# Fused attention and gated feed-forward on one core: maxima and sums of the read path in one operation for both head groups, under a new order of emission

## The chip, the cores and the metric

The kernel runs on one core of one Trainium2 chip. The metric is device time in microseconds of one execution. Before the change it is 356.61 us, the median of 3 runs (355.37 to 356.98). Engines are named as the profile names them: PE (TensorE), PEld (its weight loads), DVE (VectorE), ACT (ScalarE), POOL (GpSimd), SP (the queue that issues most transfers).

## What is computed

The reference works on x (8 batches, 8 heads, 512 positions, 64 columns) and a state of 32 rows for each batch and head, and then on both together (544 rows of 512 columns a batch) in a gated feed-forward layer:

```
scores = scale * x @ state^T ; a = softmax(scores) over the 32 state rows
xread  = a @ state
scores2 = scale * state @ x^T ; a2 = softmax(scores2) over the 512 positions
sread  = a2 @ x
y = concat([xread, sread]) with the heads side by side   # (8, 544, 512)
h = relu(y @ w_in)                                       # 1024 columns
c = convolution of 3 taps along the 544 rows, column by column
out = (h * sigmoid(c)) @ w_out
```

Softmax subtracts the row's maximum, and adds 1e-9 to the sum before it divides. The "read path" of this document is sread: the softmax over the 512 positions and its product with x.

## The kernel before

**Tiles.** A batch's scores stand transposed: 128 partitions are 4 heads of 32 state rows each, and the 8 heads make NG = 2 head groups of 512 positions. `at_b` holds both groups (128 x 2 x 512). The x path's softmax runs down the partitions in blocks of 32 on a transposed copy (`att_flip` to `att_back`); the read path's runs along the 512 positions: `top` takes each row's maximum (line 340), `exp2` the exponential with the sum as a by-product (346), `norm2` adds 1e-9 and takes the reciprocal (349, 350), `flip` and `flipped` transpose the exponentials for `read` (the product with x, 368), `divide` scales the result (375), `read_flip` and `read_flipped` put it into `sr` (379, 383). From there `state_hidden` (615) and `state_relu` (619) make the hidden columns of the state rows of four batches at a time, eight pieces f.

**The feed-forward part.** For batches 1 to 7 the hidden columns of the positions come as the product of the attention weights with (state @ w_in), in split precision: each of `a` and `u` is a high and a low part, 6 matmuls of 128x512 a piece (`hidden`, 630). Batch 0 is done in plain float32 in two halves of 256 positions (`first_scores`, `first_flip`, `first_shift`, `first_exp`, `first_sum`, `first_spread`, `first_hidden`, lines 320 and 488 to 523 and 637). `relu`, the taps `middle`, `before`, `behind` (673, 678), `sigmoid`, `gate`, `gate_high` and `gate_low` follow, and `project` (713 for two pieces of batch 0, 705 for the others) multiplies by `w_out`, 3 matmuls for each 128 positions.

**Weights.** `w_in` and `w_out` arrive as 64-bit floats in 16 pieces of 512 KB; ACT (`w_abs` 243, `w_round` 246) and DVE (`w_shift` 249, `w_sum` 252, `w_sign` 260) make 32-bit floats of each. `w_load(8)` to `w_load(15)` are the pieces of `w_out`; ACT and DVE then split them (`w_high`, `w_low`). The name in the order is `raw_j` for piece j, and `hc_j` for what `w_abs` makes of it.

**What sets the order.** Every step is added to a plan as one operation with an engine, the tokens it reads and those it writes. ORDER is a table of operation numbers; the plan emits the operations in that row. A negative number -n stands for n filler matmuls on zeros (line 215), a `v` behind a number puts an operation that ACT or DVE could do on DVE. Each engine works through its operations in the row's order and waits for the tiles that they need; a tile's buffer comes free when its last reader is done. `xx`, the x tile of `read`, has one buffer (1024 KB a batch, `x_load`, 302), `xt` four (512 KB, `xt_load`, 298), PSUM eight banks in turn. SP issues transfers in order too: one that waits holds those behind it.

Of the kernel before, what the change touches and what calls it, by code (L numbers as in the profile page):

```python
# [953 lines left out]
```

## Time and profile before

| what | value |
|---|---|
| median of 3 runs | 356.61 us |
| span of the profiled execution | 354.1 us |
| PE busy | 348.6 us (98%) |
| PEld busy | 271.8 us (77%) |
| DVE busy | 316.1 us (89%) |
| ACT busy | 256.1 us (72%) |
| granted TensorE clock, mean | 1.000 |
| transfers | 35.06 MB, mean 99 GB/s |

Busy time counts from an instruction's start to its end; instructions of one engine overlap a little, so sums of durations come out somewhat above the time that passes. The profile's chain follows the work that ended last back to the start, at each step to what released it. Stretches of the span are read on their own: the first 60 us hold the weights' conversion, batch 0 and nearly all loads, the rest is feed-forward work with the attention of later batches between it.

### The profile page before, as it was taken

How to read it: one execution, taken by the hardware profiler on the slowest of the kernel's cores; microseconds unless marked ns; L12 is line 12 of the kernel's file. 1: busy time of each engine (PE TensorE's matmuls, PEld its weight loads, DVE VectorE, ACT ScalarE, POOL GpSimd, SP SyncE). 2: the span in 40 equal slices, each digit the busy share in tenths (PEclk: the TensorE clock that was granted, in tenths of full speed). 3: DMA queues.
4: the chain of work that ended last, by engine and by line, in shares of the span. 5: the costliest groups of instructions: out<-in, count | busy, mean ns of one | idle time of the engine just before them, and what ended most of it. 6: DMA issues, size and time to landing. Idle time of an engine off the chain costs nothing.

```text
span 354.1 us, 6694 instructions
## 1 busy us (share of the span) xinstructions
PE 348.6 (98%) x2538; PEld 271.8 (77%) x2538; DVE 316.1 (89%) x563; ACT 256.1 (72%) x560; POOL 29.4 (8%) x90
## 2 busy tenths in 40 slices
PE   7999999999999999999999999999999999999995
PEld 6766758876788868878789887878788868888884
DVE  1999999999999999999999999987799898889950
ACT  3999999998777997859856657774745447548642
POOL 1000000010000000100000300042201001113000
PEclk9999999999999999999999999999999999999999
DMA  7989998201600033030400000001200011000205
GB/s 255 396 309 377 328 357 302 62 1 50 219 0 2 0 127 142 3 119 32 180 30 2 0 31 31 30 3 60 89 2 0 0 71 65 2 2 0 74 33 176
DMA packets 13584, 35.06 MB, mean 99 GB/s; under 512 B 1520, under 2 KB 4720, under 8 KB 12528
## 3 DMA queue, kind: packets, MB, share of 16 engines
q1 hardware_dynamic: 12976, 34.28, 27.1%
q8 instruction: 20, 0.33, 0.4%
q10 hardware_dynamic: 576, 0.35, 0.3%
q14 instruction: 12, 0.10, 0.1%
HBM read 25.71 MB, written 8.91 MB: 98 GB/s over the span
## 4 chain that ended last, share of the span: by engine, by line
PE 97%; DMA 2%; ACT 0%; SPq 0%; issue 0%
PE acc L705 47%; PE ps_h L630 22%; PE ps_h L637 4%; PE ps_hs L615 4%; PE ps_u L548 4%; PE acc_t L705 3%; PE ps_r L368 2%; PE ps_t L355 2%; PE ps_s L310 2%; DMA xt<-xT 2%; PE acc_c L705 2%; PE acc L713 2%; PE ps_u L567 1%; PE ps_s L498 1%; PE ps_x L498 1%; PE ps_x L512 1%
## 5 line engine op out<-in xcount | busy, mean ns | idle before, releaser
L705 PE MATMUL acc<-wo,g 128*128 128x512 f32 x726 | 177.0, 393 | 0.0
L705 PEld LDWEIGHTS acc<-wo,g 128*128 128x128 f32 x726 | 134.7, 188 | 32.8 <-issue 1.7
L630 PE MATMUL ps_h<-a,u 128*128 128x512 f32 x336 | 83.2, 391 | 0.0
L630 PEld LDWEIGHTS ps_h<-a,u 128*128 128x128 f32 x336 | 62.7, 188 | 13.1
L682 ACT ACTIVATE t<-t 128x512 f32<-128x512 f32 x64 | 39.9, 630 | 14.5 <-DVE t L678 14.3
L673 DVE SCALAR_TENSOR_TENSOR t<-h,cw,t 128x511 f32<-128x511 f32 x64 | 47.1, 742 | 1.6 <-ACT t L194 1.5
L678 DVE SCALAR_TENSOR_TENSOR t<-h,cw,t 128x512 f32<-128x512 f32 (+1 forms) x64 | 46.8, 745 | 0.6
L205 ACT ACTIVATE g<-t 128x512 fp32r<-128x512 f32 (+1 forms) x62 | 37.5, 615 | 11.0 <-DVE t L687 5.5
L687 DVE SCALAR_TENSOR_TENSOR t<-t,h 128x512 f32<-128x512 f32 (+1 forms) x64 | 42.4, 667 | 2.3 <-ACT t L682 2.2
L208 DVE TENSOR_TENSOR g<-t,g 128x512 fp32r<-128x512 f32 (+1 forms) x62 | 41.3, 671 | 3.5 <-ACT g L205 3.1
L194 ACT ACTIVATE t<-h,cw 128x512 f32<-128x512 f32 x52 | 36.9, 723 | 4.3 <-DVE h L202 3.0
L200 ACT ACTIVATE h<-ps_h 128x512 f32<-128x512 f32 x56 | 33.3, 596 | 9.3 <-PE ps_h L630 6.1
L648 POOL COPY h<-hs 128x1 f32<-128x1 f32 x40 | 14.2, 376 | 129.2 <-ACT sr L383 66.3
L205 ACT ACTIVATE u<-ps_u 128x512 fp32r<-128x512 f32 x28 | 16.2, 596 | 8.5 <-PE ps_u L548 8.5
L719 ACT ACTIVATE o<-acc 128x512 f32<-128x512 f32 (+1 forms) x30 | 15.8, 544 | 8.5 <-PE acc L705 8.3
L648 POOL COPY hs<-h 128x1 f32<-128x1 f32 x40 | 13.6, 361 | 97.6 <-ACT h L200 80.9
L208 DVE TENSOR_TENSOR u<-ps_u,u 128x512 fp32r<-128x512 f32 x28 | 18.6, 682 | 2.5 <-ACT u L205 2.5
L615 PEld LDWEIGHTS ps_hs<-sr,wi 128*128 128x128 f32 x128 | 14.8, 192 | 1.1 <-ACT t L194 0.8
L637 PE MATMUL ps_h<-p,u 128*128 128x256 f32 x64 | 15.3, 386 | 0.0
L615 PE MATMUL ps_hs<-sr,wi 128*128 128x128 f32 x128 | 15.0, 276 | 0.0
L548 PE MATMUL ps_u<-wi,st 64*32 64x512 f32 x224 | 14.3, 597 | 0.0
L637 PEld LDWEIGHTS ps_h<-p,u 128*128 128x128 f32 x64 | 11.6, 190 | 3.3 <-DVE hc L249 0.8
(99 smaller groups left out, 400.3 us busy)
## 6 DMA issues: line engine op xcount, KB each, us to landing
xt<-xT SPq DMA_DIRECT2D x16, 512.0 KB, 7.7
xx<-xn SPq DMA_DIRECT2D x8, 1024.0 KB, 5.9
out<-o SPq DMA_DIRECT2D x27, 256.0 KB, 2.1
raw<-w_in SPq DMA_DIRECT2D x8, 512.0 KB, 7.6
raw<-w_out SPq DMA_DIRECT2D x8, 512.0 KB, 7.4
out<-o SPq DMA_DIRECT2D x6, 128.0 KB, 1.8
out<-o_t SPq DMA_DIRECT2D x8, 64.0 KB, 1.7
st<-stT SPq DMA_DIRECT2D x1, 448.0 KB, 10.2
```

What stands on the lines that cost most here:

```text
L194: A.activation(dst, src, AF.Copy, scale=scale)
L200: A.activation(dst, src, AF.Relu, scale=0.5)
L205: A.activation(hi, src, AF.Copy)
L208: engine.tensor_tensor(lo, src, hi.bitcast(F32), op=ALU.subtract)
L615: PE.matmul(ps_hs[m, f][:, :NT], wi[:, k, f * P:(f + 1) * P], sr[m][:, k, :], start=(k == 0), stop=(k == NK - 1))
L630: PE.matmul(ps_h[i], u[j][:, g, fs], a[k][:, g, :], start=(n == 0), stop=(n == 3 * NG - 1))
L637: PE.matmul(ps_h[f][:, q * HS:(q + 1) * HS], us[0, f // 4][0][:, g, f % 4 * P:(f % 4 + 1) * P], half_of(pa[0], q)[:, g, :], start=(g == 0) ...
L673: V.scalar_tensor_tensor(t[:, 1:], h[:, :S - 1], cw[:, f, 0:1], t[:, 1:], op0=ALU.mult, op1=ALU.add)
L678: V.scalar_tensor_tensor(t[:, :n], h[:, 1:n + 1], cw[:, f, 2:3], t[:, :n], op0=ALU.mult, op1=ALU.add)
L682: A.activation(tt[i], tt[i], AF.Tanh, scale=0.25)
L687: V.scalar_tensor_tensor(tt[i][:, :n], tt[i][:, :n], 1.0, hd[i][:, :n], op0=ALU.add, op1=ALU.mult)
L705: PE.matmul(acc, g[j][:, cs], wo[:, k, f, :], start=(f == 0 and n == 0), stop=(f == NF - 1 and n == 2))
```

## The change

`top` and `norm2` now take both head groups of a batch in one operation: `nm2` and `s2` are tiles of two columns, one a group, and the maximum runs over `at_b` as a whole (128 x 2 x 512 to 128 x 2). `exp2` and `divide` stay one a group and read and write a column of them. With that the plan has 24 instructions fewer on DVE, the operations behind have other numbers, and ORDER is a new table.

```diff
-0 98 99 100 101 102 103 120 -9 123 121 125 -3 124 -1 142 143 126 2 -2 150 3 127 5 20 4 144 151 128 6 -1 152 132 145
+0 98 99 100 -2 101 -3 102 103 -2 120 123 125 -1 121 -2 140 2 124 126 3 141 142 143 14 -1 127 5 148 149 -1 4 144 6 15
...
-    def top(i):
-
-        b, g = divmod(i, NG)
-        nm2[i] = buf([P, 1], F32, "nm2", f"nm2_{i}")
-        V.tensor_reduce(nm2[i], at[b][:, g, :], axis=AX.X, op=ALU.max, negate=True)
+    def top(b):
+        nm2[b] = buf([P, NG], F32, "nm2", f"nm2_{b}")
+        s2[b] = buf([P, NG], F32, "s2", f"s2_{b}")
+        V.tensor_reduce(nm2[b], at[b], axis=AX.X, op=ALU.max, negate=True)
...
-        s2[i] = buf([P, 1], F32, "s2", f"s2_{i}")
-        A.activation(e2[i], at[b][:, g, :], AF.Exp, bias=nm2.pop(i), accum_out=s2[i])
-
-    def norm2(i):
-        V.tensor_scalar_add(s2[i], s2[i], EPS)
-        V.reciprocal(s2[i], s2[i])
+        A.activation(e2[i], at[b][:, g, :], AF.Exp, bias=nm2[b][:, g:g + 1], accum_out=s2[b][:, g:g + 1])
+
+    def norm2(b):
+        V.tensor_scalar_add(s2[b], s2[b], EPS)
+        V.reciprocal(s2[b], s2[b])
...
-            rows_of = [("at", b)] + [("scores", b, q) for q in ([g] if b else range(NG))]
-            add("DVE", "red", partial(top, i), r=rows_of, w=[("nm2", i)])
-            add("ACT", "exp2", partial(exp2, i), r=rows_of + [("nm2", i)], w=[("e2", i), ("s2", i)])
-            add("DVE", "norm2", partial(norm2, i), w=[("s2", i)])
+            add("ACT", "exp2", partial(exp2, i), r=rows_of + [("nm2b", b), ("s2b", b)], w=[("e2", i), ("s2", i)])
+        add("DVE", "norm2", partial(norm2, b), r=[("s2", NG * b + g) for g in range(NG)], w=[("s2b", b)])
```

The table moves instructions on every engine. Three places are shown. On PE at the start, before, the two halves of batch 0's scores (`ps_s_0_...` from the first x tile, `ps_s_0_1_...` from the second) stand ahead of both flips (`ps_x`); `idle` is the filler:

```order
L320 MATMUL ps_s_0_0_1_114<-xt_0_100,st_81 32x256
L215 MATMUL idle_102<-zeros_67 128x128 x3
L320 MATMUL ps_s_0_1_0_130<-xt_1_123,st_81 32x256
...
L320 MATMUL ps_s_0_1_1_131<-xt_1_123,st_81 32x256
L215 MATMUL idle_102<-zeros_67 128x128
L488 MATMUL ps_x_0_141<-ident_69,at_0_112 128x128 x4
L215 MATMUL idle_102<-zeros_67 128x128 x2
L488 MATMUL ps_x_1_154<-ident_69,at_0_112 128x128 x4
```

On PE at the same place, after:

```order
L320 MATMUL ps_s_0_0_1_112<-xt_0_108,st_81 32x256
L215 MATMUL idle_97<-zeros_67 128x128 x3
L488 MATMUL ps_x_0_128<-ident_69,at_0_110 128x128 x4
L320 MATMUL ps_s_0_1_0_135<-xt_1_124,st_81 32x256
...
L320 MATMUL ps_s_0_1_1_136<-xt_1_124,st_81 32x256
L498 MATMUL ps_s_0_0_0_111<-eight_74,m0_0_149 32x128 x8
L498 MATMUL ps_s_0_0_1_112<-eight_74,m0_0_149 32x128 x8
L215 MATMUL idle_97<-zeros_67 128x128
L488 MATMUL ps_x_1_177<-ident_69,at_0_110 128x128 x4
```

The first flip now stands between the halves, and single fillers are spread behind it.

On PE from `read(1)` (`ps_r_1`, x tile `xx_1`) to `read(3)` (`ps_r_3`, `xx_3`), before; `acc` is a `project`, `ps_t` a flip, and the `scores` of batch 4 stand ahead of `read(3)`:

```order
L368 MATMUL ps_r_1_702<-xx_1_697,e2t_3_668 32x64 x16
L713 MATMUL acc_0_0_735<-whole_0_630,t_0_428 128x512
...
L355 MATMUL ps_t_7_777<-ident_69,e2_7_767 128x128 x4
L705 MATMUL acc_0_2_741<-wo_80,g1_2_751 128x512
...
L705 MATMUL acc_0_1_676<-wo_80,g0_2_750 128x512 x2
L310 MATMUL ps_s_4_0_810<-xt_8_805,st_81 32x512
...
L368 MATMUL ps_r_3_828<-xx_3_826,e2t_6_820 32x64 x16
```

The same on PE after:

```order
L366 MATMUL ps_r_1_715<-xx_1_667,e2t_3_704 32x64 x16
L353 MATMUL ps_t_7_748<-ident_69,e2_7_713 128x128 x4
L713 MATMUL acc_0_1_690<-whole_1_696,t_1_404 128x512
...
L713 MATMUL acc_0_2_711<-whole_1_696,t_1_404 128x512
L705 MATMUL acc_0_0_692<-wo_80,g1_2_596 128x512
...
L705 MATMUL acc_0_1_690<-wo_80,g0_2_595 128x512 x2
L366 MATMUL ps_r_3_812<-xx_3_810,e2t_6_785 32x64 x16
L366 MATMUL ps_r_3_812<-xx_3_810,e2t_7_781 32x64 x16
L310 MATMUL ps_s_4_0_850<-xt_8_848,st_81 32x512
```

Less work of PE stands between the two reads, and the `scores` have moved behind the second.

On SP behind `x_load(3)` (`xx_3`), before:

```order
L302 DMA xx_3_826<-xn 128x2048
L298 DMA xt_10_889<-xT 128x1024
L298 DMA xt_11_891<-xT 128x1024
L239 DMA raw_14_961<-w_out 128x1024
L239 DMA raw_13_963<-w_out 128x1024
L298 DMA xt_15_965<-xT 128x1024
```

And on SP after:

```order
L302 DMA xx_3_810<-xn 128x2048
L298 DMA xt_8_848<-xT 128x1024
L298 DMA xt_13_888<-xT 128x1024
L239 DMA raw_13_890<-w_out 128x1024
L298 DMA xt_12_895<-xT 128x1024
L239 DMA raw_15_897<-w_out 128x1024
L239 DMA raw_14_933<-w_out 128x1024
```

`raw_14` has moved from the third place behind `x_load(3)` to the sixth.

On ACT around `w_abs(14)` (`hc_14`), after; `hs` are the copies out of `ps_hs`:

```order
L243 ACTIVATE hc_14_935<-raw_14_933 128x512
L246 ACTIVATE raw_13_890<-raw_13_890 128x512
L246 ACTIVATE raw_14_933<-raw_14_933 128x512
L243 ACTIVATE hc_15_943<-raw_15_897 128x512
L205 ACTIVATE wo_80<-whole_4_916 128x512
L619 ACTIVATE hs_83<-ps_hs_0_6_927 128x4x32
L619 ACTIVATE hs_83<-ps_hs_0_2_904 128x4x32
```

On ACT there, before:

```order
L619 ACTIVATE hs_83<-ps_hs_0_2_948 128x4x32
...
L619 ACTIVATE hs_83<-ps_hs_0_5_933 128x4x32
L243 ACTIVATE hc_14_988<-raw_14_961 128x512
L682 ACTIVATE t_6_909<-t_6_909 128x512
L194 ACTIVATE t_7_997<-h_7_871,cw_78 128x512
```

`w_abs(14)` now stands ahead of most copies out of `ps_hs`, where it stood behind five of the eight.

## Rows read from the trace of the kernel before

**Rows 1.** The page: busy us and share by engine; shares of the chain.
```profile
PE 348.6 (98%) x2538; PEld 271.8 (77%) x2538; DVE 316.1 (89%) x563; ACT 256.1 (72%) x560; POOL 29.4 (8%) x90
...
PE 97%; DMA 2%; ACT 0%; SPq 0%; issue 0%
```

**Rows 2.** Stretches: us; busy of PE, PEld, DVE, ACT, POOL; clock, DMA share, GB/s.
```profile
20.00:40.00 20.00, 20.00 (x277) 14.12 (x277) 19.88 (x39) 19.73 (x46) 0.00 (x0) 1.00 0.95 340
40.00:60.00 20.00, 19.96 (x247) 12.54 (x246) 18.85 (x40) 19.02 (x47) 0.00 (x0) 1.00 0.97 359
```

**Rows 3.** The chain in order of time: start us, us, engine, tile, line, instructions.
```profile
7.84 0.42 PE idle L215 x2
...
10.65 0.42 PE idle L215 x2
...
242.43 2.72 PE ps_h L630 x12
...
350.57 0.66 ACT o L719 x2
```

**Rows 4.** The timeline of PE at the start; in brackets idle time and its releaser.
```profile
7.17 0.67 PE L320 MATMUL ps_s<-xt,st 64*32 64x256 f32 x16 [0.57 <-DMA xt<-xT]
```

**Rows 5.** Groups by line on DVE: busy us, mean ns of one, idle before.
```profile
L340 DVE TENSOR_REDUCE nm<-at 128x1 f32<-128x512 f32 x16 | 10.8, 679 | 0.0
L437 DVE TENSOR_REDUCE m<-af 128x32 f32<-128x1024 f32 x7 | 8.5, 1215 | 0.1
...
L350 DVE RECIPROCAL s<-s 128x1 f32<-128x1 f32 x16 | 2.6, 164 | 0.5
...
L349 DVE TENSOR_SCALAR s<-s 128x1 f32<-128x1 f32 x16 | 2.3, 144 | 0.0
```

**Rows 6.** The chain again: single pieces of PE's work between 27 and 65 us.
```profile
27.89 1.03 PE ps_r L368 x64
...
32.14 3.46 PE ps_h L637 x16
...
38.76 0.87 PE ps_t L355 x8
...
41.47 0.86 PE acc L713 x2
42.33 1.02 PE ps_s L310 x16
...
57.49 7.34 PE ps_hs L615 x64
```

**Rows 7.** Transfers and a stretch: SP's issue; issues with median us to landing (at 44.5, 154.2, 131.3, 51.8, 52.2 us).
```profile
44.54 0.33 SPq L302 DMA_DIRECT2D xx<-xn  x1
...
xx<-xn SPq DMA_DIRECT2D x1, 1024.0 KB, 7.5
...
xx<-xn SPq DMA_DIRECT2D x1, 1024.0 KB, 4.9
...
xx<-xn SPq DMA_DIRECT2D x1, 1024.0 KB, 5.6
...
raw<-w_out SPq DMA_DIRECT2D x1, 512.0 KB, 4.1
raw<-w_out SPq DMA_DIRECT2D x2, 512.0 KB, 5.5
...
50.00:52.00 2.00, 2.00 (x22) 0.93 (x20) 2.00 (x4) 2.00 (x5) 0.00 (x0) 1.00 0.99 399
```

**Rows 8.** Groups by line on ACT: busy us, mean ns of one, idle before.
```profile
L246 ACT ACTIVATE raw<-raw 128x512 uint32<-128x512 uint32 x16 | 11.4, 720 | 0.0
L243 ACT ACTIVATE hc<-raw 128x512 f32<-128x512 f32 x16 | 11.2, 708 | 0.0
...
L205 ACT ACTIVATE wo<-whole 128x512 fp32r<-128x512 f32 x8 | 5.1, 635 | 0.4 <-DVE whole L260 0.4
...
L619 ACT ACTIVATE hs<-ps_hs 128x128 f32<-128x128 f32 x16 | 4.2, 273 | 4.1 <-PE ps_hs L615 4.1
```

More of the change, by code (lines that the diff above doesn't have):

```diff
@@ new lines @@
+1543 1544 1058 1545 1546 1054 1069 1084 398 1082 1094 1095 1068 1083 1531 394 400 1108 1081 1109 1110 1112v 1098 1113
+1114 1097 1102 1123 1099 1532 1533 1103 1096 1115 1116 1138 1124 1127v 1125 1534 1117 1104 1535 1118 1119 1121 1139
+1128 1129 1130 1120 1536 1537 1122 1100v 1101 1131 1153 1142v 1538 1539 1140 1143 1144 1547 1111 1548 1132 1088 1133
+1154 1156 1136 1549 1073 1137 1157v 1135 1155 1145 1146 1158 1159 1147 1148 1160 1106 1161 1550 1134 1107 362 363 364
+365 1149 1150 1551 1552 1151 1152 366 1168 395 1162 1163 1166 1167 1169v 1170 1171 1553 1172v 1173 1174 1175 1176 1164
@@ new lines @@
+1183 1184 1185 1165 1198 1177 1554 1141 1555 1187 1178 1182 1181 1179 1199 1200 1202 1180 1188 1189 1203 1556 1190
+1191 1192 1204 1193 1205 1201 1557 1206 1213 1214v 1558 1194 1207 1197 1208 1217v 1559 1196 1560 1561 433 1562 1195
+1210 1211 1212 1215 1218 1219 1569 1220 1221 1563 1209 1564 1567 1566 1222 1223 1105 1236 1237v 1240v 1568 1565 1238
+1241 1251 1252 1255 1242 1243 1256 1224 1228 1229 1126 1226 1225 1227 1244 1245 1234 1253 1257 1258 1246 1266 1267
+1259 401 1248 1268 402 404 1270v 1260 1230 1271 1272 1247 1249 1250 1261 1263 1281 1264 1269 1265 403 1273 1274 1275
@@ new lines @@
+1282 1285 434 1283 405 1276 1262 1254 1231 1278 1279 1280 1286 1287 1296 1288 1289 1570 1290 1277 1291 1294 1293 1292
+1297 1300v 1301 1295 1232 1298 1302 1239 1303 1304 1299 1305 1306 1326 1327 1330 1216 1311 1307 1310 1331 1328 1341
+1312 1315v 1342 1313 1316 1343 1317 1332 1344 1318 1319 435 436 437 438 439 1320 1321 1233 1333 1334 440 1345 441 1309
+1308 1364 1322 1324 1335 1323 1346 1347 1336 1325 1340 1186 1365 1348 443 1349 1368 1366 1367 1571 1350 1338 1339 1369
+1370 1572 1573 1351 1371 1372 1574 1575 1577 1578 1337 1352 1356v 1373 1374 1379 1380 1383v 1384 1576 1284 1381 1385
@@ new lines @@
+1386 1355 1357 1382 1579 1580 1362 444 1353 1581 1582 1387 1388 1375 1376 1354 1583 442 1585 1586 1394 1389 1395 1397
+1377 1398v 1399 1378 1390 1393 1396 1587 1588 1235 1400 1589 1590 1401 1402 1392 1391 1409 1403 1410 1411 1413 1314
+1591 1358 1359 1593 1584 1592 1424 1425 1404 1408 1414 1594 1412 1595 1407 1405 1596 1415 1428v 1406 1597 1426 1416
+1429 1598 1599 1600 1360 1417 1418 1430 1431 1609 1439 1440 1442 1441 1419 1420 1432 1454 1610 1433 1443v 1421 1611
+1434 1435 1436 1455 1457 1612 1444 1445 1427 1613 1458 1459 1446 1447 1614 1615 1423 1438 1456 1460 1601 1602 1448
@@ L121 @@
+1449 1461 1469 1470 1462 1463 1471 1422 1453 1437 1452 1473v 1603 1604 1451 1474 1329 1605 1475 1606 1607 1476 1464
+1477 1617 1618 1619 1478 1479 1608 1616 1468 1620 1621 1361 1622 1623 1625 1363 1466 1481 1472 1483 1488 1496 1626
+1627 1497 1628 1490v 1629 1489 1630 1498v 1499 1491 1467 1482 1494 1495 1631 1492v 1493 1624 1632 1633 1634 1635 1637
+1636 1450 1465 1480 1486 1484 1485 1487
 """
@@ L374, in divide @@
             rr[b] = buf([P, NG, D], F32, "rr", f"rr_{b}")
-        A.activation(rr[b][:, g, :], ps_r[b][:, g * D:(g + 1) * D], AF.Copy, scale=s2.pop(i))
+        A.activation(rr[b][:, g, :], ps_r[b][:, g * D:(g + 1) * D], AF.Copy, scale=s2[b][:, g:g + 1])
     def read_flip(b):
@@ L400, in attention @@
                 w=[("scores", b, g)] + [("at", b)] * (b > 0 and g == 0))
+        rows_of = [("at", b)] + [("scores", b, q) for q in range(NG)]
+        add("DVE", "wide", partial(top, b), r=rows_of, w=[("nm2b", b), ("s2b", b)])
         for g in range(NG):
             i = NG * b + g
-            rows_of = [("at", b)] + [("scores", b, q) for q in ([g] if b else range(NG))]
-            add("DVE", "red", partial(top, i), r=rows_of, w=[("nm2", i)])
-            add("ACT", "exp2", partial(exp2, i), r=rows_of + [("nm2", i)], w=[("e2", i), ("s2", i)])
-            add("DVE", "norm2", partial(norm2, i), w=[("s2", i)])
+            add("ACT", "exp2", partial(exp2, i), r=rows_of + [("nm2b", b), ("s2b", b)], w=[("e2", i), ("s2", i)])
+        add("DVE", "norm2", partial(norm2, b), r=[("s2", NG * b + g) for g in range(NG)], w=[("s2b", b)])
+        for g in range(NG):
+            i = NG * b + g
             add("PE", "flip", partial(flip, i), r=[("e2", i)], w=[("ps", "t", i)])
@@ L411, in attention @@
         for g, i in enumerate(pair):
-            add("ACT", "rr", partial(divide, i), r=[("ps", "r", b), ("s2", i)] + [("rr", b)] * g,
+            add("ACT", "rr", partial(divide, i), r=[("ps", "r", b), ("s2b", b)] + [("rr", b)] * g,
                 w=[("rq", b, g)] if g else [("rq", b, g), ("rr", b)])
```

30 lines of the change are left out of this document (8 added, 22 removed), and 68 rows, old and new, of the table ORDER.

## The prediction

> **What bounds the kernel now.** I read the page's busy line and chain first, then the busy time by stretch. TensorE (PE) is busy 98% of the span, and 97% of the chain that ended last is PE's own work, with nothing of VectorE (DVE) in it [rows 1]. The reader is to see that it is real work back to back and not waiting that looks busy: a `hidden` group of 12 matmuls takes 2.72 us at 242 us, 227 ns each, and the last PE work ends at 350.57 us, when the two last evacuations begin [rows 3]. From the second half of the first x tile at 7.17 us on [rows 4], PE has work in every slice.
>
> The second look is at the others, because a PE without slack stops as soon as one of them is late. From 20 to 60 us four resources are full at once: PE 20.0 of 20 in either half, DVE 19.9 and 18.9, ScalarE (ACT) 19.7 and 19.0, and the DMA share is 0.95 and 0.97 [rows 2]. Over the whole span DVE is at 89% and ACT at 72% [rows 1], so behind this stretch they have more room. The granted clock is 1.00 in both stretches, the upper level (2.4 GHz). So this is a kernel whose time is PE's work (some 343 us from 7.17 to 350.57) plus a start of 7.2 us and a tail of 3.5 us, and the one stretch in which a new order can easily go wrong is 20 to 60 us.
>
> **The arithmetic that is merged.** The 16 maxima of 128x512 (679 ns each, 10.9 us) become 8 of 128x1024. The nearest row for one of those is the max over the same number of elements in L437, 1215 ns, so 9.7 us: 1.1 us less. The 16 pairs of add and reciprocal on one column (144 + 164 ns, 4.9 us) become 8 pairs on two columns; at the same price that is 2.5 us less [rows 5]. Together DVE loses 3.6 us of its 316. ACT keeps its 16 exponentials; they only read a column of a two-column tile. Four more operations carry the mark that puts them on DVE (29 instead of 25), most of them `middle`, where two engines can do the step. All of this lies beside PE's work, which is not shortened by a single matmul: I put it at zero. The cover is PE's 98%; were it gone, the 3.6 us would show in full, and that is a rival below.
>
> The merge also adds a wait. A maximum of batch b now waits for the copies of both head groups out of PSUM (before, `at_2`'s first maximum stood ahead of the second copy's end), and both exponentials wait for that one maximum. Behind it on DVE stand `w_sign` and the taps. The new order places other work ahead of it, so I bound this by zero and by 0.68 us a batch, the maximum that could run during the second copy [rows 5], less the 0.45 us (3.6 / 8) that each batch's merge gives back: some 0.2 us for each of the four batches inside the full stretch, 0.9 us, all of it on DVE, which is not on the path. Zero in the sum.
>
> **The start.** PE now flips the first half of batch 0 (4 transposes, 0.44 us) between the two halves of the scores, where before it ran fillers and waited 0.57 us for the second half of x [rows 3, 4]. That work was after 7.84 us before; it is now in the wait: -0.4 us. Between zero (the copy that it needs ends too late to fit) and -0.4. Fillers stay at 16; three pieces of them, of which the first and the last stand in [rows 3], cost 0.42 to 0.45 us of chain each before, 1.3 us in all. After, six single ones stand behind the scores, about 0.2 us each, again 1.3 us: zero, and up to -1.3 if what they wait for is early.
>
> **The reads and the transfers.** This is the part that I think decides. `x_load(3)` may be issued only when `read(1)` has ended, since `xx` has one buffer. Before, between `read(1)` and `read(3)` PE did five `project` steps on whole weights and two on split ones, three flips, and a `scores`, 8.9 us from read to read, and the load, issued at 44.54 us, landed 7.5 us later, just in time. After, the order has read(1), flip, three `project` on whole weights, three on split ones, then `read(3)`: 1.03 + 0.44 + 3 x 0.86 + 0.11 + 3 x 0.68 = 6.2 us from start to start, so 5.2 us from the end of `read(1)` [rows 3, 6, 7]. A load of 1024 KB in an empty queue took 4.9 to 5.6 us [rows 7]. Both ways out: 0 to 0.6 us of waiting at `read(3)`.
>
> When is that? The PE steps ahead of `read(0)` are the same set in both orders; it started at 27.9 us before, so 27.5 now. Up to `read(1)` the new order has 2 reads (1.03), 3 groups of 1.02 (a block, two `scores`), 5 flips (0.44), 8 `first_hidden` (0.865), 3 `project` (0.86) and two single flips (0.1): 17.1 us [rows 6]. So `read(1)` is at 44.6, ends at 45.6, and `read(3)` is due at 50.8. The load lands at 50.5 to 51.2; by the bytes, 512 KB fewer stand ahead of it than before, so 52.0 less 1.3 gives 50.7 [rows 7].
>
> Then the queue: behind `x_load(3)` stand, in the new order, `xt_load(8)`, `xt_load(13)`, `w_load(13)`, `xt_load(12)`, `w_load(15)` and `w_load(14)`, six loads of 512 KB. At the best rate of this stretch (399 GB/s at 50 to 52 us, 1.31 us a load) `w_load(14)` lands at 58.7; at that of 20 to 40 us (340 GB/s, 1.54 us) at 60.0 [rows 2, 7]. ACT takes `w_abs(14)` in its turn, and behind it in ACT's queue stand two roundings, one more `w_abs`, one high part and two copies of `ps_hs`: 0.71 + 0.72 + 0.72 + 0.71 + 0.63 + 2 x 0.27 us, less some 0.12 us of overlap each, 3.3 us [rows 8]. The last of these copies frees the bank that `scores(6)` writes, so PE waits for it. PE is due there 1.03 + 1.02 + 0.1 + 3 x 0.68 + 7 x 0.92 = 10.6 us after `read(3)` begins [rows 3, 6], at 61.4. So `w_load(14)` must land by 58.0, and comes at 58.7 to 60.0: 0.7 to 2.0 us late, the wait at `read(3)` contained in it. Before, `w_load(14)` went out ahead of `w_load(13)` and three x loads (issued at 51.8 us and landed 4.1 us later, at 55.9 [rows 7]), and ACT came to it behind five of the eight copies of `ps_hs`. I take 1.0, nearer the fast end, because the rate of 340 has the gated gaps of the early weights in it; the ends stay 0 (if ACT is behind its turn anyway, it waits for nothing) and 2.0.
>
> The Trainium skill (Perfetto Trace Analysis, section Engine Utilization) gives 358 GB/s as 100% of a core's memory bandwidth. By that a load of 512 KB would take 1.46 us, `w_load(14)` would land at 59.5 and this term would be 1.5 instead of 1.0. The rows disagree: 399 GB/s over two whole microseconds is above it, so I keep the rows.
>
> **The sum.** The profiled execution has a span of 354.1 us; the runs shown have a median of 356.6, that is 2.5 us around it, which I leave as it is. 354.1 + 0 (merged arithmetic) - 0.4 (start) + 1.0 (transfers) = 354.7 of span, and 357.2 us for the median.
>
> **Rivals.** *Slower: the transfers are late by more.* Same place, `w_load(14)` before `scores(6)`. Before, two `w_out` loads were issued 0.4 us apart at 51.8 and 52.2 us; one took 4.1 us and the pair's middle was 5.5, so the other took 6.9: a piece can come 1.5 us behind its turn of 1.3 [rows 7]. With that on top of 60.0 it lands at 61.5, 3.5 us late: 356.6 - 0.4 + 3.5 = 359.7. For it speaks a DMA share of 0.97 over the stretch; against it, that the new order issues the first weights with fewer gates. It decides from a landing after some 60.2 us on, where the sum passes +0.5%.
>
> *Faster: everything fits.* Transfers in time, and the six fillers' places need no waiting: -0.4 - 1.3, 354.9 us. For it speaks that DVE and ACT have less to do; against it, that the copies and maxima of batch 0 still follow the second half of x, which lands when it did.
>
> *The relief reaches the path.* If PE had headroom and DVE set the pace, all 3.6 us would come back: 353.0 us. For it, DVE is at 97% from 20 to 60 us [rows 2]; against it, the chain has no DVE in it and matmul groups follow each other at 227 ns. The Trainium skill (Perfetto Trace Analysis, section Identifying the Most-Contended Engine) says that matmul busy time is a poor measure of how near PE is to its limit, and that busy time of the weight loads is the better one: here 77%, below DVE's 89% [rows 1], and by that rule this rival would be the forecast. The trace speaks against it here: the pitch of 227 ns holds in groups without any wait.
>
> **How the numbers follow.** Forecast 0.62, late transfers 0.24, everything fits 0.09, relief on the path 0.05. Within 0.5% (1.8 us, about what a measurement of this kernel can tell from no change) lies the forecast, nearly whole, and half of "everything fits": 0.65. Slower by more: late transfers and 0.02 of the forecast, 0.26. Faster: the relief and the other half of "everything fits", 0.09. The range: from 355.4 (the forecast's lower end: start -0.4, transfers 0, most of the fillers' time saved) to 360.0 (late transfers, with a third of the 0.9 us for the added wait on DVE).
>
> **What would show it.** In the profile after: 8 maxima at about 1.2 us and a DVE busy sum near 313 us (the merge); the first flip ahead of 7.17 us (the start); a wait of PE's weight loads at `read(3)`, near 51 us, on a transfer, and at `scores(6)`, near 61 us, on ACT's copy out of `ps_hs`, with ACT idle before `w_abs(14)` on a transfer (the reads). If PE shows no such wait, the transfer term is wrong; if PE waits on DVE from 20 to 120 us, the added wait was not free; if the granted clock leaves 1.00, PE had longer holes than I allow.

## The result: 1.0% slower, and where the profile after shows it

| | before | after |
|---|---|---|
| median of the runs, us | 356.58 (355.37 to 359.24, 10 runs) | 360.67 (359.14 to 362.44, 10 runs) |
| ratio, 95% interval | 1 | 1.0104 (1.0080 to 1.0128) |
| span of the profiled execution, us | 354.1 | 359.6 |

In a second comparison the changed kernel's ratio was 1.0086 (1.0063 to 1.0109). I had forecast 357.2 us and "within 0.5%" as the likeliest; it is 3.5 us more, and outside the range.

The page after, busy us by engine and shares of the chain, answers to [rows 1]:

```profile
PE 350.6 (98%) x2538; PEld 272.5 (76%) x2538; DVE 320.4 (89%) x543; ACT 258.0 (72%) x556; POOL 30.8 (9%) x90
...
PE 92%; DMA 5%; ACT 2%; issue 0%; DVE 0%
```

PE is still busy for 98% of the span, but 8% of the chain is no longer PE's (3% before): a transfer and ACT stand in it. DVE, which has twenty instructions fewer, makes 0% of it. The next view, the longest waits from 40 to 80 us of the kernel after (engine, line, waited for: us, times, longest), says which:

```profile
ACT hc L243 <- DMA raw<-w_out: 2.9, 1, 2.9
PEld ps_s L310 <- ACT hs L619: 2.9, 1, 2.9
PE ps_s L310 <- ACT hs L619: 2.7, 1, 2.7
```

ACT waits 2.9 us for `w_load(14)`, and PE 2.7 us for a copy that stands behind it on ACT. The timelines of ACT and of PE (start us, us, what; in brackets the idle time and its releaser) place both:

```profile
59.13 0.59 ACT L619 ACTIVATE hs<-ps_hs 128x128 f32<-128x128 f32 x2
62.61 0.66 ACT L243 ACTIVATE hc<-raw 128x512 f32<-128x512 f32 x1 [2.90 <-DMA raw<-w_out]
...
65.36 0.91 ACT L619 ACTIVATE hs<-ps_hs 128x128 f32<-128x128 f32 x5
```

```profile
65.67 1.92 PE L310 MATMUL ps_s<-xt,st 64*32 64x512 f32 x16 [2.70 <-ACT hs L619]
66.98 2.32 PE L548 MATMUL ps_u<-wi,st 64*32 64x512 f32 x16
68.69 1.64 PE L310 MATMUL ps_s<-xt,st 64*32 64x512 f32 x16
```

`w_abs(14)` begins at 62.61, 3.1 us later the copies are through, and `scores(6)` begins at 65.67. The three PE groups behind the hole take 1.92, 2.32 and 1.64 us, where the same work elsewhere takes 1.10, 1.07 and 1.20. The windows of that stretch (us; busy of PE, PEld, DVE, ACT, POOL; granted clock, DMA share, GB/s) show why:

```profile
62.00:64.00 2.00, 0.97 (x9) 0.78 (x7) 0.69 (x2) 1.39 (x3) 0.00 (x0) 1.00 0.32 129
64.00:66.00 2.00, 0.33 (x8) 0.30 (x16) 2.00 (x4) 2.00 (x8) 0.00 (x0) 1.00 0.02 8
66.00:68.00 2.00, 2.00 (x25) 1.04 (x19) 1.86 (x4) 0.62 (x3) 0.00 (x0) 0.53 0.00 0
68.00:70.00 2.00, 2.00 (x32) 0.61 (x16) 0.71 (x2) 2.00 (x4) 0.00 (x0) 0.62 0.54 178
```

After PE had stood still, the granted clock is 0.53 and 0.62 over two windows: most of them at the lower level, 1.2 of 2.4 GHz. From the start of the first to the end of the third they take 1.7 us more than the same three in the last kernel of section 4 (68.69 + 1.64 - 65.67 = 4.66 against 64.89 + 1.20 - 63.15 = 2.94). With the wait that is 4.4 of the 5.5 us of span. So the first reading was: a late load, an in-order queue on ACT, a hole, and the clock behind it, much as the slower rival had it. It names the place in this one execution; the experiments show that the place changes, and that the cause lies further up. Nor does the clock make the median: of the ten executions two, this one among them, have a mean granted clock of 0.995; the other eight have 0.998 to 1.000 and still take 359.1 to 361.3 us.

### The profile page after: what moved, and what is told of

Same layout as the page of the kernel before. It is cut to its first block, busy times and chain, and to the rows that moved or that the text cites. A ratio compares the mean times of both kernels' runs of the same rounds, so it can differ in the third digit from the quotient of the medians.

```text
span 359.6 us, 6675 instructions
## 1 busy us (share of the span) xinstructions
PE 350.6 (98%) x2538; PEld 272.5 (76%) x2538; DVE 320.4 (89%) x543; ACT 258.0 (72%) x556; POOL 30.8 (9%) x90
## 4 chain that ended last, share of the span: by engine, by line
PE 92%; DMA 5%; ACT 2%; issue 0%; DVE 0%
PE acc L705 45%; PE ps_h L630 21%; PE ps_u L548 4%; PE ps_h L637 4%; DMA raw<-w_out 3%; PE acc_t L705 3%; PE ps_hs L615 2%; PE ps_t L353 2%; PE ps_r L366 2%; PE ps_s L310 2%; PE acc_c L705 2%; DMA xt<-xT 1%; PE idle L215 1%; PE acc L713 1%; PE ps_u L567 1%; PE ps_s L498 1%
## 5 line engine op out<-in xcount | busy, mean ns | idle before, releaser
L705 PE MATMUL acc<-wo,g 128*128 128x512 f32 x726 | 175.0, 393 | 0.0
L205 ACT ACTIVATE g<-t 128x512 fp32r<-128x512 f32 (+1 forms) x62 | 38.4, 622 | 20.1 <-DVE t L687 19.4
L673 DVE SCALAR_TENSOR_TENSOR t<-h,cw,t 128x511 f32<-128x511 f32 x64 | 47.3, 745 | 2.6 <-ACT t L194 1.8
L200 ACT ACTIVATE h<-ps_h 128x512 f32<-128x512 f32 x60 | 35.9, 598 | 14.2 <-PE ps_h L630 13.2
L194 ACT ACTIVATE t<-h,cw 128x512 f32<-128x512 f32 x45 | 32.5, 723 | 0.6
L648 POOL COPY h<-hs 128x1 f32<-128x1 f32 x40 | 16.2, 419 | 88.0 <-DVE t L687 80.5
L548 PE MATMUL ps_u<-wi,st 64*32 64x512 f32 x224 | 15.8, 631 | 0.0
L243 ACT ACTIVATE hc<-raw 128x512 f32<-128x512 f32 (+1 forms) x17 | 11.4, 669 | 5.2 <-DMA raw<-w_out 2.9
```

Of the source, the lines that this page charges most:

```text
L194: A.activation(dst, src, AF.Copy, scale=scale)
L200: A.activation(dst, src, AF.Relu, scale=0.5)
L205: A.activation(hi, src, AF.Copy)
L548: PE.matmul(ps_u[b, hf, g][j * NS:(j + 1) * NS, :], st[half, b * NP + j, :], wi[half, j, hf * 512:(hf + 1) * 512], start=True, stop=True)
L673: V.scalar_tensor_tensor(t[:, 1:], h[:, :S - 1], cw[:, f, 0:1], t[:, 1:], op0=ALU.mult, op1=ALU.add)
L705: PE.matmul(acc, g[j][:, cs], wo[:, k, f, :], start=(f == 0 and n == 0), stop=(f == NF - 1 and n == 2))
```

## Experiments

Short names in the diffs are the planned operations, in the order of the engine named; ratios are to the kernel before on the same chip.

### 1. The merge or the order?

Theory A: the late `w_load(14)`. Theory B: the merged operations cost, or the loss is spread over the new order.

e3, the merge alone in the old order:

```diff
 DVE (order of before)
-top(2b) ... top(2b+1)        norm2(2b) ... norm2(2b+1)
+top(b), at the first place   norm2(b), at the first place
```

> The order of the kernel before, with only the maxima and the sums of both head groups in one operation each (each at the place of the first of the two, for batches 2 and 3 behind the second copy of scores). Theory A: the merge is hidden work on VectorE, 356.6 us, ratio to before 0.997 to 1.003, VectorE about 3 us less busy. Theory B (the merge costs, because exp2 of one head group waits for the maximum over both): over 358 us.

Measured: ratio 1.0001 (0.9974 to 1.0027). On DVE 16 maxima of 10.8 us became 8 of 9.7, 32 small steps of 4.9 us became 16 of 2.6.

e4, the new order with the maxima and sums apart again:

```diff
 DVE (order of after)
-top(b)                 norm2(b)
+top(2b), top(2b+1)     norm2(2b), norm2(2b+1)
```

> The order of the changed kernel, with the maxima and sums split again into one operation for each head group, both at the merged one's place. Theory A (order alone): the same 2.9 us wait of ScalarE for w_load(14) near 60 us, the same hole before scores(6) and half clock behind it: 360.7 us (359.7 to 361.7), ratio to before 1.008 to 1.014. Theory B (the merge costs): 356.6 us.

Measured: 1.0109 (1.0069 to 1.0149). Its profiled execution, the shortest of the six (span 356.9 us), has the two waits at less than half their size, 1.3 us on ACT and 1.1 us on PE, and no lower clock. So, to the 0.3% that e3 can tell, the merge is free and worth nothing, and the order alone makes the loss. That is shown; theory B falls as to the merge.

### 2. Is it the late `w_load(14)`?

e9 puts it still later:

```diff
 SP
+xt_load(11)
+xt_load(10)
 w_load(14)
-xt_load(11)
-xt_load(10)
```

> The changed kernel with w_load(14) put still later: xt_load(11) and xt_load(10) are issued ahead of it; nothing else moves. Theory A: w_load(14) lands near 65.1 instead of 62.6 us, ScalarE's wait, the start of scores(6) and the end of the kernel move by the same 2.5 us, and the half clock comes in more of the runs: 360.7 + 2.5 = 363.2 us (362.2 to 365), ratio to before 1.015 to 1.024. Were the late load not on the path of the timed runs: 360.7, ratio 1.010.

Measured: 1.0218 (1.0186 to 1.0250), 364.36 us. Its profiled execution, the longest wait from 40 to 80 us and two windows:

```profile
ACT hc L243 <- DMA raw<-w_out: 3.6, 1, 3.6
```

```profile
68.00:70.00 2.00, 2.00 (x33) 0.98 (x33) 1.90 (x4) 1.26 (x4) 0.00 (x0) 0.74 0.04 12
70.00:72.00 2.00, 2.00 (x24) 0.36 (x8) 1.12 (x3) 2.00 (x4) 0.00 (x0) 0.50 0.70 248
```

`w_load(14)` landed at 64.6 us, 2.0 us later than in the changed kernel, and the profiled span is 2.0 us longer (361.6 against 359.6): one to one. The median rose by more (ratio 1.0218 against 1.0104), with a mean granted clock of 0.991 in four of the six executions. So this place can set the time. Whether it is what did so in the changed kernel is another question, and two repairs ask it:

```diff
 SP (e1)                     ACT (e2)
 xt_load(8)                  state_relu(0,3)
+w_load(13)                 +state_relu(0,6)
+w_load(14)                 +state_relu(0,2)
+w_load(15)                  w_abs(14)
 xt_load(13)                 ...
-w_load(13)                 -state_relu(0,6)
 xt_load(12)                -state_relu(0,2)
-w_load(15)
-w_load(14)
```

> Edit to the changed kernel: the transfers w_load(13), w_load(14) and w_load(15) are issued ahead of xt_load(13) and xt_load(12); nothing else moves. Theory A (the transfer): w_load(14), which landed at 62.6 us, lands at about 57.7 (the second place in the row of landings 55.5, 57.7, 60.2), before ScalarE reaches w_abs(14) at 59.7; ScalarE's 2.9 us of idle time, the 2.86 us hole of TensorE before scores(6) and the stretch at half clock behind it (1.55 us) go together: 360.7 - 4.4 = 356.3 us (355.5 to 357.3), granted clock 1.00 from 66 to 70 us. xt_load(12) lands near 62.6, just when scores(6) is due (62.8). Theory B (the time lies in the merged operations or spread over the new order): no more than 1 us goes, 359.7 to 360.7. Theory C (the link is simply too full before 62 us): scores(6) then waits for xt_load(12) instead, about 359.

> Edit to the changed kernel: on ScalarE the two copies state_relu(0,6) and state_relu(0,2) stand ahead of w_abs(14) instead of behind w_high(4); the transfers keep their places. Theory A in its narrow form (what costs is the place of the copies behind a wait, not the late load itself): w_load(14) still lands at 62.6 us and ScalarE still waits for it, but scores(6) has its bank and starts at about 62.8 instead of 65.7; granted clock 1.00; 356.3 us (355.5 to 357.3). If the late load itself holds TensorE in another way (weights of chunk 6 needed soon after), a hole appears later and 358 to 360 us remain. Theory B (merged operations or the order at large): 359.7 to 360.7.

> The kernel of e2 (copies first) once more, on the chip of e10, e11 and the changed kernel: ratio to before 1.004 to 1.009, as measured; the profiled run tells how far the hole before read(3) varies (1.85 us in the first).

Measured: e1 1.0076 (1.0051 to 1.0101), e2 1.0065 (1.0040 to 1.0089) and again 1.0077 (1.0053 to 1.0102). Between a tenth and little more than a third of the loss came back, by which of the two ratios of the changed kernel is taken, and the intervals reach into those of the changed kernel. The timeline of PE in e2 shows a repaired place and a new hole ahead of it:

```profile
53.75 1.10 PE L366 MATMUL ps_r<-xx,e2t 128*32 128x64 f32 x64 [1.68 <-DMA xx<-xn]
...
64.61 1.09 PE L310 MATMUL ps_s<-xt,st 64*32 64x512 f32 x16
```

`scores(6)` starts with no wait, but `read(3)` has waited 1.68 us for `x_load(3)`. In e1 the same, and `scores(4)` waits for its x load besides:

```profile
53.58 1.10 PE L366 MATMUL ps_r<-xx,e2t 128*32 128x64 f32 x64 [1.24 <-DMA xx<-xn]
55.42 1.09 PE L310 MATMUL ps_s<-xt,st 64*32 64x512 f32 x16 [0.74 <-DMA xt<-xT]
```

Then the changed kernel itself, profiled once more:

> The changed kernel itself on the same chip: ratio to before 1.008 to 1.013, as measured. The profiled run tells how far its hole before scores(6) (2.86 us in the first) and the stretch at half clock (there in the first) vary from one execution to the next: theory A expects the hole to follow the landing of w_load(14), ScalarE's w_abs(14) starting at it and scores(6) 3.1 us behind.

Measured: 1.0086 (1.0063 to 1.0109), span 359.1. Its PE timeline and a window:

```profile
53.29 1.10 PE L366 MATMUL ps_r<-xx,e2t 128*32 128x64 f32 x64 [0.73 <-DMA xx<-xn]
55.81 1.73 PE L310 MATMUL ps_s<-xt,st 64*32 64x512 f32 x16 [1.42 <-DMA xt<-xT]
```

```profile
56.00:58.00 2.00, 2.00 (x18) 0.53 (x3) 0.70 (x2) 0.01 (x1) 0.00 (x0) 0.53 0.97 377
```

Here is no hole before `scores(6)` at all. The holes lie ten microseconds earlier, the lower clock follows them, and the span is the same to 0.5 us. `w_load(14)` landed at 62.6 us in both executions, but here PE and ACT came to it late already, and nothing waited for it. Theory A falls as the whole cause: the place of the hole changes between the two executions, the price hardly. What the holes have in common is a load that has not landed.

### 3. Filling the hole before `read(3)`

Theory D: what is left is PE standing before `read(3)`. All three of these have e2's copies first as well.

```diff
 PE (e6)                  PE (e7)                  PE, SP (e10)
 project(2,1)             project(0,0)             project(2,1)
+project(3,0)            +read(1)                 +scores(4)
+project(3,1)             flip(6)                  read(3)
 read(3)                  project(0,2)            -scores(4)
 scores(4)               -read(1)                 xt_load(9)
 read_flip(3)             flip(7)                 +xt_load(8)
-project(3,0)                                      x_load(3)
-project(3,1)                                     -xt_load(8)
```

e8 is e6 and e7 together; e11 is e1, e2 and e10 together.

> The kernel with the two copies first (e2), and project(3,0) and project(3,1) moved ahead of read(3) on TensorE (their inputs are there at 49 us); nothing else. Theory D: what is left of the loss lies before read(3), whose x_load(3) lands at 53.6 us, two microseconds after it is due, because its transfer waits for the end of read(1), which stands two microseconds later in the new order. 1.6 us of other work then stands in the hole of 1.85 us: read(3) still starts near 53.7, but nothing idles; 359.7 - 1.5 = 358.2 us (357.4 to 359.0), ratio to before 1.001 to 1.005. Theory E (the rest lies in the long second part, from 80 us on, or is spread): no gain, 359.3 to 360.

> The kernel with the two copies first (e2), and read(1) moved on TensorE ahead of flip(6) and project(0,2) (its x_load(1) has landed at 44.1 us); nothing else. Theory D: read(1) ends near 45.4 instead of 46.7 us, x_load(3) is issued 1.3 us earlier, lands near 52.3 instead of 53.6, and the hole before read(3) shrinks from 1.85 to about 0.6 us: 358.5 us (357.7 to 359.3), ratio to before 1.002 to 1.006. If the full link and not the issue sets the landing, x_load(3) still lands at 53.6 and nothing is gained: 359.7.

> The edits of e6 and of e7 together with the two copies first (e2). Theory D: no hole over 0.4 us on TensorE between 40 and 75 us, granted clock 1.00 in nearly every run; 357.8 us (357.0 to 358.7), ratio to before 0.999 to 1.004: the changed order is then worth no more than the old one. What is left over before would be the 1 us that TensorE loses between 80 us and the end. Were the new order better apart from its two holes, under 356.5.

> The kernel with the two copies first (e2), and scores(4) moved ahead of read(3) on TensorE, with its transfer xt_load(8) issued ahead of x_load(3) on the queue; nothing else. Theory D in its second form (the rest of the loss is TensorE standing before read(3) for x_load(3); the cover has to be work that is ready, which project(3,0) and project(3,1) were not): scores(4) fills 1.1 us of the 1.85 us, nothing behind it waits that did not wait before; ratio to before 1.002 to 1.005, 0.2 to 0.4% under e2 beside it. Theory E (the rest lies elsewhere, or x_load(3) lands later because xt_load(8) goes first): the ratio of e2, 1.005 to 1.009.

> The edits of e1 (w_load(13) to w_load(15) ahead of xt_load(13)), e2 (copies first) and e10 (scores(4) and its transfer first) together. Theory D in its second form, with the late load gone as well: ratio to before 1.001 to 1.004, the best of the repaired ones. Theory E: 1.005 to 1.009. Were the new order better than the old one apart from its two holes, under 0.998.

Measured: e6 1.0091 (1.0067 to 1.0114), e7 1.0062 (1.0036 to 1.0089), e8 1.0084 (1.0065 to 1.0102), e10 1.0076 (1.0046 to 1.0106), e11 1.0087 (1.0056 to 1.0117). None is below e2 by more than its interval: five misses. In e6 I had overlooked an input, the low half of chunk 3's weights, and the work that I moved was also the cover of what came behind:

```profile
53.61 1.42 PE L705 MATMUL acc<-wo,g 128*128 128x512 f32 x5 [1.25 <-DVE wo L208]
...
59.04 1.16 PE L615 MATMUL ps_hs<-sr,wi 128*128 128x128 f32 x8 [1.00 <-ACT sr L381]
```

In e7, the best of the five, the profiled execution (the second shortest of ten) has no wait at `read(3)`. In e10 the work was ready, and the wait for `x_load(3)` was there all the same:

```profile
55.74 1.10 PE L366 MATMUL ps_r<-xx,e2t 128*32 128x64 f32 x64 [1.17 <-DMA xx<-xn]
```

But e10 also put `x_load(3)` behind another load: it landed at 55.6 us, against 53.6 in e2, so e10 can't tell whether the cover would have been enough. What stays is a wait for transfers.

### 4. The one buffer of `x_load`

Theory F: `xx` has one buffer, so `x_load(1)` may go out only when `read(2)` has ended and `x_load(3)` only when `read(1)` has, and SP's queue stands still behind each. Theory G: the link is simply full. SP's timeline of the kernel after (`x_load(1)`, `x_load(3)`), and of the kernel before (`x_load(1)`):

```profile
39.03 0.33 SPq L302 DMA_DIRECT2D xx<-xn  x1
...
46.52 0.33 SPq L302 DMA_DIRECT2D xx<-xn  x1
```

```profile
36.89 0.33 SPq L302 DMA_DIRECT2D xx<-xn  x1
```

In the new order `read(2)` begins at 37.94 and takes 1.03 us (the chain after, next fence), in the old one it began at 35.70, so the load goes out 2.1 us later. `x_load(3)` goes out 2.0 us later (before: [rows 7]).

```profile
37.94 1.03 PE ps_r L366 x64
```

The window 38 to 40 us, first after, then before:

```profile
38.00:40.00 2.00, 2.00 (x81) 1.07 (x78) 1.97 (x4) 2.00 (x6) 0.00 (x0) 1.00 0.04 16
```

```profile
38.00:40.00 2.00, 2.00 (x15) 1.82 (x14) 2.00 (x4) 2.00 (x6) 0.00 (x0) 1.00 0.66 231
```

In the middle of a stretch that is full of transfers the link moved 16 GB/s for two microseconds. PE, DVE and ACT were all full there, which is why no wait is to be seen at 39 us. I took this pause for what is paid at 51 to 66 us; the landings below do not bear that out.

f1 takes the first of the two waits away, shortens the second, and moves no instruction but a memset on POOL:

```diff
-xxs[b] = buf([P, NCH, DM], F32, "xx", f"xx_{b}")
+if b == 1:   # the state tokens' tile, empty until state_relu(0,0)
+    xxs[b] = every.rearrange("p a l w -> p (a l w)")[:, :NCH * DM].rearrange("p (c d) -> p c d", d=DM)
+else:
+    xxs[b] = buf([P, NCH, DM], F32, "xx", f"xx_{b}")
 ...
-G.memset(every[:, :, :, W - 1:], 0.0)      # at the start
+G.memset(every[:, :, :, W - 1:], 0.0)      # at the end of read(1)
```

`x_load(3)` then waits for `read(2)` instead of `read(1)`. f2 is this edit in the kernel before, f4 in e2, g2 in e3.

> The changed kernel and its order, word for word, but x_load(1) writes into the tile of the state tokens (every), which is empty until state_relu(0,0); its last column is zeroed behind read(1) on GpSimd. So x_load(1) no longer waits for read(2), and x_load(3) waits for read(2) (end at 39 us) instead of read(1) (end at 46.5). Theory F (the one buffer xx turns over too slowly for the new order, in which read(2) and read(1) stand two microseconds later; the queue stands still behind each x_load, and every load behind it, w_load(14) too, is late): the queue no longer stands still near 39 us, x_load(1) lands near 41.5 instead of 44, x_load(3) near 48 to 50 instead of 52 to 53.5, w_load(14) before 60; no hole over 0.5 us on TensorE from 40 to 80 us, no half clock; 360.3 - 4 = 356.3 us, ratio to before 0.996 to 1.003. Theory G (the link is full from 40 to 65 us and the loads could not come earlier whatever the buffer does; or the loss is in TensorE's own order): ratio 1.005 to 1.010 as in the repaired ones.

> The kernel before with the same edit (x_load(1) into the tile of the state tokens). Its order has only 1.2 us of holes between 40 and 80 us, 0.4 of it at read(1) for x_load(1). Theory F: up to 0.7 us is gained, ratio 0.997 to 1.000. If the edit itself costs something (the zeros behind read(1), the earlier transfer in the way of others), over 1.002.

> f1 with the two copies first (e2) as well. Theory F: with the loads on time the place of the copies no longer matters: as f1 within 0.3%, ratio 0.996 to 1.003. If w_load(14) is still late in some executions, this one is 0.2 to 0.4% under f1.

> f1 (the changed kernel with x_load(1) into the tile of the state tokens) once more, for a second profiled run and the ratio: 1.000 to 1.003 as measured, no idle stretch of the link from 38 to 42 us, and no hole over 0.5 us on TensorE between 54 and 80 us; the hole at read(3) (1.2 us in the first profiled run, which was the slowest of its twelve) under that.

Measured: f1 1.0014 (0.9995 to 1.0033), again 1.0025 (1.0005 to 1.0044); f4 1.0022 (0.9997 to 1.0048); f2 0.9984 (0.9966 to 1.0002). Freeing one buffer gives back between seven and nine tenths of the loss. In the old order the same edit gives nothing clear of noise (f2, and g2 below), so it is no gain of its own. f4 can't be told from f1: with the buffer freed the place of the copies no longer shows. The second profiled execution of f1, its window, SP's issues of `x_load(1)` and `x_load(3)`, and PE's timeline:

```profile
38.00:40.00 2.00, 2.00 (x76) 1.40 (x82) 1.97 (x4) 1.97 (x7) 0.00 (x0) 1.00 1.05 430
```

```profile
31.83 0.44 SPq L305 DMA_DIRECT2D hs<-xn  x1
...
42.39 0.38 SPq L305 DMA_DIRECT2D xx<-xn  x1
```

```profile
52.51 1.10 PE L369 MATMUL ps_r<-xx,e2t 128*32 128x64 f32 x64
...
63.15 1.10 PE L313 MATMUL ps_s<-xt,st 64*32 64x512 f32 x16
64.04 1.07 PE L553 MATMUL ps_u<-wi,st 64*32 64x512 f32 x16
64.89 1.20 PE L313 MATMUL ps_s<-xt,st 64*32 64x512 f32 x16
```

The link is full at 38 us, `x_load(3)` goes out at 42.39 instead of 46.52, and neither `read(3)` nor `scores(6)` waits. The first profiled execution of f1, the longest of its twelve, still had a wait of 1.0 us at `read(3)`: `x_load(3)`, issued at 43.5 us, landed only at 54.4, and `w_load(14)` at 62.3. An early issue does not always bring an early landing, so theory G has a part in what is left.

Which of the two turns is it? The transfers' issues with their time to landing, for `xt_load(9)` (the load right ahead of `x_load(3)`), `x_load(3)` and `w_load(14)`, in the second profile of the changed kernel and then in the second of f1:

```profile
xt<-xT SPq DMA_DIRECT2D x1, 512.0 KB, 6.8
...
xx<-xn SPq DMA_DIRECT2D x1, 1024.0 KB, 5.9
...
raw<-w_out SPq DMA_DIRECT2D x1, 512.0 KB, 11.1
```

```profile
xt<-xT SPq DMA_DIRECT2D x1, 512.0 KB, 7.1
...
xx<-xn SPq DMA_DIRECT2D x1, 1024.0 KB, 9.2
...
raw<-w_out SPq DMA_DIRECT2D x1, 512.0 KB, 8.5
```

A landing is the issue plus that time. With the starts of `read(0)` and `scores(6)` from PE's timelines, all in us:

| profile | `read(0)` | `xt_load(9)` landed | `x_load(3)` issued, landed | `w_load(14)` landed | `scores(6)` | `read(0)` to `scores(6)` | span |
|---|---|---|---|---|---|---|---|
| changed kernel | 27.9 | 48.0 | 46.5, 51.9 | 62.6 | 65.7 | 37.8 | 359.6 |
| again | 28.6 | 48.5 | 47.3, 53.2 | 62.6 | 67.0 | 38.4 | 359.1 |
| e2 | 28.1 | 48.0 | 46.8, 53.6 | 62.4 | 64.6 | 36.5 | 357.0 |
| e7 | 28.3 | 48.5 | 46.5, 52.3 | 61.2 | 63.6 | 35.3 | 355.9 |
| f1 | 29.6 | 50.7 | 43.5, 54.4 | 62.3 | 65.5 | 35.9 | 357.9 |
| f1 again | 28.6 | 49.1 | 42.4, 51.6 | 59.3 | 63.2 | 34.5 | 355.2 |

All that the loads cost is made by `scores(6)`: from its start to the end thirteen of the fifteen profiles in the new order take 292.1 to 292.5 us, the two with the lower clock behind `scores(6)` (the first of the changed kernel, and e9) 293.9. The changed kernel and f1, each profiled again, are a pair: `read(0)` starts at 28.62 in both, `read(1)` at 46.12 and 46.13, and `scores(6)` 3.85 us apart, as are the spans (3.9).

The landings do not show that PE pays for the pause at 38 to 40 us. Wherever the new order leaves `read(1)` at its place, it starts 17.5 to 17.7 us after `read(0)`, with the pause or without, so it never waited for `x_load(1)`; and `xt_load(9)` landed no later in the changed kernel than in f1. What f1 gains lies behind that load. In its second profile `x_load(3)` is in the queue by then and lands 2.6 us behind it (3.7 in the first, long one); in the changed kernel it goes out late, because `read(1)` has to end first, and lands 3.9 and 4.7 us behind. The six loads from there to `w_load(14)` take 10.7 and 9.4 us, in f1 7.9 and 7.6. So the traces point to the second turn, `x_load(3)` behind `read(1)`, and e7, which brings `read(1)` forward, has the shortest way to `scores(6)` of all that lack f1's edit. No run frees one turn alone in the new order: the buffer is shown as the cause, the turn is read from landings. Why the six loads come more slowly is open: windows of these profiles with a DMA share of 0.97 and more go from 248 GB/s (changed kernel, 52 to 54 us) to 438 (first of f1, 40 to 42 us).

The other way round, the first turn alone put late in the kernel before:

```diff
 PE, ACT (order of before)
-read(2)
 first_hidden(6,1)
 first_hidden(7,0)
 flip(3)
-divide(4), divide(5)
 flip(2)
+read(2)
+divide(4), divide(5)
```

> The kernel before with one thing of the new order put into it: read(2) (and the two scaled copies of its result, divide(4) and divide(5)) stands behind first_hidden(6,1), first_hidden(7,0), flip(3) and flip(2), at about 38.5 instead of 35.7 us; the order of the transfers is untouched. Theory F: x_load(1) is issued 2.8 us later, at 39.7; the loads ahead of it have landed by 39.5 us, so the link stands idle for 1.5 to 2 us there; x_load(1) lands near 45.3, read(1), due at 43.4, waits some 2 us for it, and nothing behind gives it back: ratio to before 1.004 to 1.007. Were the place of read(2) without weight: 0.998 to 1.002.

Measured: 1.0028 (1.0009 to 1.0047), 358.17 us. Window and PE timeline of g1:

```profile
38.00:40.00 2.00, 2.00 (x69) 1.76 (x69) 2.00 (x4) 1.28 (x4) 0.00 (x0) 1.00 0.05 20
```

```profile
44.15 1.10 PE L368 MATMUL ps_r<-xx,e2t 128*32 128x64 f32 x64 [1.10 <-ACT t L682]
...
53.92 1.10 PE L368 MATMUL ps_r<-xx,e2t 128*32 128x64 f32 x64 [0.80 <-ACT t L194]
```

The same pause of the link (20 GB/s), and PE stops at both reads, 1.10 and 0.80 us. (The brackets name ACT steps that came last by the profile; `x_load(1)`, issued at 39.2 us and 4.8 us under way, landed at 44.0, just ahead of `read(1)`; `x_load(3)`, issued at 45.3, landed at 53.8, just ahead of `read(3)`.) Here the pause is not made up: `xt_load(9)` landed at 51.3 us, against 49.6 in the kernel before. So a late first turn can cost as well, in the old order 0.28%: less than I expected, and about a third of the changed kernel's loss. That the loss stays small because `w_load(14)` goes out earlier there (it landed at 57.5) is argued, not shown.

> The merged operations in the order of before (e3), with x_load(1) into the tile of the state tokens (the edit of f1 and f2). Theory F: as f2, ratio to before 0.996 to 1.001; the merge adds and saves nothing. It is the candidate for the fastest of these kernels.

Measured: 1.0011 (0.9994 to 1.0029). Nothing here beats the kernel before beyond doubt; f2 comes nearest, and its interval reaches past 1.

## Why the prediction was wrong, point by point

**What bounds the kernel** was right. PE is 98% busy, and the work it does is the same 2538 instructions. That 20 to 60 us is the stretch where a new order goes wrong was nearly right: the loads come late from 46 us on, and what PE loses to them it has lost by `scores(6)`, at 63 to 67 us.

**The merged arithmetic at zero** was right, by e3. Of the 3.6 us less on DVE, the rows after show 3.4 (mean ns of one in the last column but one; they answer to [rows 5]):

```profile
L339 DVE TENSOR_REDUCE nm<-at 128x2 f32<-128x1024 f32 x8 | 9.7, 1214 | 0.8 <-ACT at L194 0.6
...
L348 DVE RECIPROCAL s<-s 128x2 f32<-128x2 f32 x8 | 1.3, 165 | 0.3
L347 DVE TENSOR_SCALAR s<-s 128x2 f32<-128x2 f32 x8 | 1.3, 161 | 0.0
```

The maximum of 1024 columns took 1214 ns, as the row of L437 had said (1215). But DVE's busy sum rose to 320.4 where I had looked for 313. The page counts overlapping instructions once: added up one by one DVE's instructions fell from 355.1 to 352.5 us, and they overlap less in the new order. That sign of mine was badly chosen. **The added wait** at zero was right as far as e3 and e4 can tell, and **the relief on the path** was not there. The rule of the Trainium skill that I had weighed with it (Perfetto Trace Analysis, section Identifying the Most-Contended Engine) judges PE by the busy share of its weight loads and by a second measure, its matmul work against its peak, which I did not work out. By the weight loads alone DVE would have been the engine to relieve; e3 relieved it by 3.4 us and gained nothing, so that half of the rule did not hold here.

**The start, -0.4**, came as described but gave nothing: the first flip stands ahead of the second half's scores, and `read(0)` still began at 27.85 us, as before (27.82, both from PE's timeline), not at 27.5. Over all profiles it was worse than nothing: in the fifteen of the new order `read(0)` begins at 27.85 to 29.58 us, 28.6 in the mean, in the five of the old order at 27.62 to 28.38, 28.0 in the mean. Why is not known.

**The transfers, +1.0**, is the step that failed, and by its size. The mechanism was the right one: `x_load(3)` has to wait for `read(1)`, the loads behind it come late, and PE pays at `read(3)` or at `scores(6)`. Every figure on the way was too small:

- `read(1)` ended, and `x_load(3)` went out, at 46.5 us (47.3 in the second profile), not at 45.6: the start gave nothing, and from `read(0)` to `read(1)` PE took 17.5 us, not 17.1.
- `x_load(3)` landed at 51.9 us (53.2), not at 50.5 to 51.2. The sentence "by the bytes, 512 KB fewer stand ahead of it than before, so 52.0 less 1.3 gives 50.7" counts a queue that never runs low; here the load ahead landed 1.5 us (1.2) after `x_load(3)` went out.
- The six loads behind it took 1.79 us each (1.57), where 1.31 to 1.54 were counted. So `w_load(14)` landed at 62.6 us in both profiles, not at 58.7 to 60.0.

That made a wait of 2.7 us at `scores(6)` in the first profile, where the sum had 1.0, and 1.7 us of lower clock, which the sum had at nothing. From `read(0)` to `scores(6)` PE took 3.3 us more than in the second profile of f1, which has no wait there, and 3.9 us more in the second profile, lower clock contained. Of the signs that I had named, the wait at `scores(6)` and ACT idle before `w_abs(14)` were there in the first profile, the wait at `read(3)` for a transfer in the second. I had not asked about `x_load(1)` and its wait for `read(2)`, the same rule one turn earlier; the pause of the link that it makes is real, but in the new order the landings show nothing paid for it.

**The slower rival** had the place of the first profile and nearly the size (359.7 us; a landing at 61.5, which was 62.6), but gave as its cause a single piece 1.5 us behind its turn (its rows give 1.9, since the second piece was issued 0.4 us later). What the profile shows is `x_load(3)` late by 1.2 us and three loads behind it that took 2.2 to 2.5 us each. That its number came so near is in part luck, and it sat at one instruction, while the second profile paid at another.

**The clock** was in my list of signs and not in the sum. In the first profiled execution it made 1.7 us of 5.5, but only two of the ten executions show it. The 358 GB/s of the Trainium skill (Perfetto Trace Analysis, section Engine Utilization), which I set aside for 399, is what that section calls 100% of a core's share; it also says that one core alone can pull more, up to some 435. The windows of f1, 430 and 438, are close to that. But the best rate did not decide here: the six loads of the changed kernel came at 294 GB/s.

**Still open:** the 0.14 to 0.25% that f1 keeps, of which only one interval excludes zero (beside the same edit in the old order the medians differ by 0.3%, f2, and 0.1%, g2; the later `read(0)`, 0.6 us in the mean, would be 0.2%); which of the two turns of the buffer costs how much; and why the loads behind `x_load(3)` come at different rates.

## What to carry to other kernels

When a new order moves the last reader of a single buffer, look for the load that waits for it and at every load that stands behind that one in the queue: what comes late is paid microseconds later, at a place that changes from one execution to the next. A repaired wait that comes back elsewhere says to look upstream of both. A pause of the link is not yet a price: follow the landings load by load, before and after, to the first load from which on nothing is made up. Two profiles in which PE runs alike up to some point show best what comes behind it. Making an operation cheaper on an engine with cover was worth nothing here, but the order that came with it was worth a sum of its own.
